# Places of two groups of SBUF tiles written out in tables instead of left to pools of three and of six

## The chip, the cores and the metric

One core of a Trainium2 chip runs the kernel. The metric is device time in microseconds (us) of one execution; lower is better. The engines are named as the profile names them: PE (matrix products; PEld is its weight load), DVE (vector), ACT (scalar), POOL (GpSimd) and SP, whose queue issues all the DMAs of this kernel in the order of the program.

## The reference

A recurrent attention over 768 steps feeds a gated dense part (batch 4, 8 heads of 40, model width 320, inner width 1024):

```python
for t in range(S):                       # state: [B, H, 40, 40]
    y[:, :, t] = einsum('bhd,bhde->bhe', r_t, state)
    Sa = einsum('bhde,bhe->bhd', state, a_t)
    state = state * w_t - einsum('bhd,bhe->bhde', Sa, b_t) + einsum('bhd,bhe->bhde', v_t, k_t)
x = y as [batch, time, 320]
h = gelu_tanh(x @ w_in); u, v = halves of h
v_n = (v - mean) / sqrt(var + 1e-6) * g_ln
v_s = einsum('ts,bsd->btd', w_sg, v_n) + b_sg
out = x + (u * v_s) @ w_out
```

All is 32-bit floating point, with `w_in` and `w_out` handed over as 64-bit numbers.

## The kernel before

**Attention.** Time is cut into 12 chunks of 64 steps. For each chunk the gates, a triangular inverse of size 64 and a chain of small products over the four batches run. The inverse is a long row of small products and sums `th<-x,n`, `x<-x,th` on POOL (tiles `tg` and `th` in turn from chunk to chunk), finished by a few instructions on DVE (`x<-x,n`) and two transposes (`x1z<-x`, `xt<-x1z`). Results go to DRAM (`xd<-yt`), from where the dense part reads them.

**Dense part.** It starts while the last chunks of the attention run. Its weights come first: `split64` (lines 1026 to 1066) takes one block of 128 x 256 numbers of 64 bits through these steps: `load` (DMA into a stage tile `stg`), `size` (ACT, `sc<-stg`), `fields` and `scale` (DVE, on `sc`, `lt`, `stg`), `parts` (ACT, `lt<-lt` and `wih<-stg`), `low` (three instructions on DVE or on POOL, the last of them `wil<-stg,lt`). `weights_in` lists twelve such blocks of `w_in`, `part_out` eight of `w_out`. The end of `low` is the last use of a block's stage tile.

**Order.** Every instruction is kept in program order on its engine (class `InOrder`), so ACT, DVE, POOL and SP each work through a fixed list, and an instruction that waits holds up all that stands behind it. Times in tables place each step in that list: `DEC` gives each of the twelve blocks its time and whether DVE (0) or POOL (1) does `low`; `DSTEP` gives the distances of its six steps:

```python
DSTEP = ((-15.76, -2.54, -1.13, -0.3, 1.65, 2.2), (-13.56, -0.46, 1.98, 3.41, 7.44, 12.01))
DEC = ((268.49, 0), (278.24, 0), (290.42, 0), (291.86, 0), (282.12, 1), (294.83, 1), (305.79, 1), (316.12, 0),
    (310.87, 0), (320.78, 1), (326.62, 0), (327.2, 1))
```

Sorted by the time of `load`, the blocks are those with index 0, 1, 4, 2, 3, 5, 6, 8, 7, 9, 10, 11. So POOL does `low` of the third, sixth, seventh, tenth and twelfth block that is loaded, DVE that of the others.

**Places.** A stage tile comes from `stage` (line 1007), out of a group of three equal places; the temporary tiles (`sc`, `lt` of `split64`; `p`, `q` of `gelu2`) come from `tmp` (line 1004), out of six. A new tile has to wait until the tile that had its place before is used for the last time. Which place a tile gets is decided where the program is put together, not in the source. There are 20 stage tiles and 152 temporary ones. The banks of PSUM are given out otherwise: class `Banks` reads the place of each tile from a table, `BANK`.

Of the kernel before, what the change touches and what calls it, by code (L numbers as in the profile page):

```python
# [24 lines left out]
HF = DF // 2  # L25
# [94 lines left out]
    1000.0, 1000.0, 1000.0)  # L120
HEADX = (1000.0, 13.61, -7.08, 1000.0, 4.3, 5.34, 13.95, 11.71, 1000.0, 1000.0, 6.17, 4.08, 1000.0, 8.27, 26.21, 8.84,
    3.72, 15.74, 23.09, 1000.0, 10.42, -4.32, 14.21, 1000.0)
BANK = ("0123450123435501250453111055152145231023102310214320321405302453145321045301502402315034310243524305"
        "1243154102103541323510234023145023452410413524303541032103425103235034134250321253412041230541202512"
        "3423051204052340134021534015412312054103051230423014523040530120145304245012431240351243523013045234"
# [13 lines left out]
class Banks:  # L139


    def __init__(self, tc, ctx):
        self.tc, self.ctx, self.n = tc, ctx, 0
        self.pools = [self.bank(i) for i in range(6)]
# [13 lines left out]
    def __call__(self, nm):  # L158
        k = int(BANK[self.n]) if self.n < len(BANK) else self.n % len(self.pools)
        self.n += 1  # L160
        return self.pools[k].tile([128, 512], F32, tag="ps", name=nm)
# [17 lines left out]
def engines(tc):  # L179
    nc = tc.nc  # L180
    return tuple(InOrder(tc, e) for e in (nc.vector, nc.scalar, nc.gpsimd, nc.tensor, nc.sync))
# [6 lines left out]
def attention(tc, a, xd, flag, keep, ps, mlp=None):  # L188
# [4 lines left out]
    with ExitStack() as ctx:  # L193
# [586 lines left out]
        def loads(f, stage, c, bs, *a):  # L780
            assert all((stage, c, b) in seen for b in bs)
            f(*a)
# [147 lines left out]
class Mlp:  # L930
# [3 lines left out]
    def __init__(self, tc, ps, xd, w_in, w2, g_ln, wst, b_sg, w_out, out):  # L934
        self.tc, self.ps, self.xd, self.out = tc, ps, xd, out
        self.w_in, self.w2, self.g_ln, self.wst, self.b_sg, self.w_out = w_in, w2, g_ln, wst, b_sg, w_out
        self.V, self.A, self.G, self.T, self.Q = engines(tc)
        self.ctx = ExitStack()
        self.vn, self.us, self.gs, self.xin, self.left, self.outs = {}, {}, {}, {}, [8] * B, {}
        self.ready = set()  # L940
        self.n, self.todo, self.plan, self.hold, self.held = 0, [], None, None, {}
# [60 lines left out]
        self.ut.update({(f, 1): p.tile([128, 384], F32, name=f"u{4 + f}") for f in range(4)})  # L1002

    def tmp(self, nm, n, dt=F32):
        return self.sb.tile([128, HF], dt, name=nm, tag="pq", bufs=6)[:, 0:n]

    def stage(self, n, dt):
        return self.sb.tile([128, HF], dt, name="stg", tag="stg", bufs=3)[:, 0:n]

    def later(self, *steps):  # L1010

# [314 lines left out]
    def run(self, ahead, verdict=None):  # L1326

        done = [(x, b) for x, b, _ in FILL] if ahead else []
        seq, jobs = [], []
        if not ahead:  # L1330
            self.ps.grow()
            self.open_in()
            for g in self.weights_in():
                for f in g(self.G):
                    f()
            self.open_x()
            self.open_v()
            self.open_sg()
        self.open_rest()
        for b in range(B):  # L1340
            seq += [(x, b + (x[0] in "uvx")) for x in (SEQL if b == B - 1 else SEQ)] if b else list(SEQ0)
        seq = [x for x in seq if x[1] < B and x not in done and (ahead or x[0][0] != "j")]
        for i, (x, b) in enumerate(seq):
            if x[0] == "x" and (b or not ahead) and not (ahead and (x, b) == ("x0", 1) and PX1):
                jobs.append((max(0, i - XL), lambda b=b, n=int(x[1]): self.load_x(b, n)))
            if verdict and (x, b) == ("s7", 1):
                jobs.append((i, lambda: self.later((8, 9, verdict()))))
        rest, loads, parts, wo = self.weights_rest([(i % 6, i // 6) for i, _ in SGA] if ahead else [])
        jobs += [(REST - 3, rest[0]), (REST, rest[1])]
        for k, f in enumerate(loads):  # L1350
            if f:
                jobs.append((SGS[k - 5] if k > 4 else 0, f))
        for k, f in enumerate(parts):
            if f:
                jobs.append((SGS[k], f))
        for k, g in enumerate(wo):
            for d, f in zip(OSTEP, g):
                jobs.append((OUTS[k] + d, f))
        jobs.sort(key=lambda x: x[0])
        for i, (x, b) in enumerate(seq):  # L1360
            while jobs and jobs[0][0] <= i:
                jobs.pop(0)[1]()
            self.piece(x, b)
        self.flush()
        self.ctx.close()
# [111 lines left out]
```

## Time and profile before

| | |
|---|---|
| median of 3 runs | 610.83 us (609.41 to 615.5) |
| the profiled execution | 612.37 us |
| its span, first to last instruction | 610.6 us |
| mean granted clock of PE | 0.959 |
| busy share: PE, DVE, POOL, ACT | 93%, 80%, 60%, 59% |
| chain that ended last, by engine | PE 62%, DVE 16%, POOL 7%, ACT 5%, issue 4%, DMA 3% |

The profile is that of one execution. Busy shares are means over the whole span. The page also gives the busy share in 40 slices of 15.3 us: PE stands at nine tenths or more in most of them, at six tenths in the slice from 305 to 321 us. The chain that ended last is followed back from the last instruction, at each step to what released it. "SPq" is SP's queue of DMAs.

### The profile page before, as it was taken

Reading aid. Unit: us, or ns where it says so; the run is one execution under the profiler, and the core shown is the slowest. Engines: PE = TensorE matmul, PEld = TensorE weight load, DVE = VectorE, ACT = ScalarE, POOL = GpSimd, SP = SyncE. Lnnn points to the kernel's source line nnn. Section 1 sums busy time; section 2 is a strip of 40 time slices with the busy share of each in tenths; the row PEclk is TensorE's granted clock in tenths of the full one; section 3 lists DMA queues with packets and bytes.
Section 4 is the critical chain, followed back from the end, with each engine's and each line's share of the span. In section 5 each row is a group of like instructions: output and inputs, shape, how many; then the busy total and the mean of one; then the engine's idle time right before and its main releaser. Section 6 shows DMA issues by size and latency. Waiting matters only on the chain.

```text
span 610.6 us, 23787 instructions
## 1 busy us (share of the span) xinstructions
PE 566.4 (93%) x9784; PEld 515.1 (84%) x9784; DVE 489.5 (80%) x1083; ACT 359.0 (59%) x993; POOL 363.5 (60%) x844
## 2 busy tenths in 40 slices
PE   6777999999999999999968989699999999999996
PEld 5666888888888888888857879699899999999996
DVE  7868999999989999997846887898887779568733
ACT  5546788797787887976826737444453246224410
POOL 7648888888888798888871344355433332333230
PEclk9875999999999999999897999799999999999999
DMA  5522335444454345525405415500121103010002
GB/s 204 151 66 83 91 100 138 132 122 120 123 138 126 98 127 137 137 73 139 123 10 149 113 51 158 166 29 5 34 73 38 34 1 110 2 33 13 20 1 71
DMA packets 56886, 54.01 MB, mean 88 GB/s; under 512 B 35840, under 2 KB 47360, under 8 KB 56768
## 3 DMA queue, kind: packets, MB, share of 16 engines
q1 hardware_dynamic: 56768, 52.40, 30.7%
q8 instruction: 79, 1.29, 0.9%
q14 instruction: 39, 0.32, 0.2%
HBM read 44.52 MB, written 7.86 MB: 86 GB/s over the span
## 4 chain that ended last, share of the span: by engine, by line
PE 62%; DVE 16%; POOL 7%; ACT 5%; issue 4%; DMA 3%; SPq 0%; DVEq 0%; POOLq 0%; ACTq 0%
PE sg L174 12%; PE ru L174 8%; PE ab L174 7%; PE op L174 6%; PE hu L174 6%; PE pq L174 5%; PE yp L174 5%; PE hv L174 4%; PE sp L174 3%; POOL x L174 3%; DVE at L174 2%; POOL th L174 2%; PE ut L174 2%; DVE fixed L174 2%; DVE ex L174 2%
## 5 line engine op out<-in xcount | busy, mean ns | idle before, releaser
L174 POOL TENSOR_TENSOR th<-x,n 128x126 f32<-128x126 f32 (+21 forms) x174 | 65.5, 376 | 21.6 <-DVE n L174 10.5
L174 POOL TENSOR_TENSOR x<-x,th 128x126 f32<-128x126 f32 (+21 forms) x174 | 69.1, 397 | 8.2
L174 PE MATMUL sg<-wsh,vh 128*128 128x384 f32 x192 | 66.0, 344 | 4.5 <-ACT wsh L174 4.5
L174 POOL TENSOR_TENSOR gx<-g,gy 128x384 fp32r<-128x384 f32 x30 | 31.8, 1063 | 64.5 <-ACT gy L174 64.5
L174 PE MATMUL sg<-wsl,vh 128*128 128x384 f32 x192 | 65.8, 342 | 0.4 <-POOL wsl L174 0.4
L174 PE MATMUL sg<-wsh,vl 128*128 128x384 f32 x192 | 65.7, 342 | 0.0
L174 POOL TENSOR_TENSOR tg<-x,n 128x126 f32<-128x126 f32 (+25 forms) x160 | 57.3, 358 | 12.3 <-DVE n L174 5.0
L174 POOL TENSOR_TENSOR x<-x,tg 128x126 f32<-128x126 f32 (+25 forms) x160 | 60.2, 376 | 7.1
L174 PE MATMUL pq<-rt,vut 128*64 128x128 f32 x768 | 52.6, 278 | 1.2 <-issue 1.1
L174 PE MATMUL ab<-at,kb 64*64 64x64 f32 x1536 | 39.6, 233 | 11.3 <-POOL kb L174 3.6
L174 ACT CAST gy<-g 128x384 fp32r<-128x384 f32 x30 | 15.4, 514 | 55.4 <-DVE g L174 52.7
L174 PEld LDWEIGHTS pq<-rt,vut 128*64 128x64 f32 x768 | 43.3, 139 | 3.9 <-issue 2.2
L174 ACT CAST vh<-v 128x512 fp32r<-128x512 f32 x24 | 14.9, 621 | 53.3 <-DVE v L174 53.3
L174 PEld LDWEIGHTS ab<-at,kb 64*64 64x64 f32 x1536 | 32.7, 141 | 15.3 <-POOL kb L174 4.0
L174 DVE TENSOR_TENSOR at<-ab,mask 64x256 f32<-64x256 f32 x96 | 40.4, 421 | 5.4 <-PE ab L174 2.9
L174 POOL TENSOR_TENSOR vl<-v,vh 128x512 fp32r<-128x512 f32 x24 | 31.5, 1311 | 20.8 <-ACT vh L174 20.8
L174 PEld LDWEIGHTS sg<-wsh,vh 128*128 128x128 f32 x192 | 37.0, 193 | 5.3 <-ACT wsh L174 4.8
L174 DVE SCALAR_TENSOR_TENSOR g<-sg,gl,bt 128x384 f32<-128x384 f32 x32 | 19.7, 615 | 25.3 <-PE sg L174 24.2
L174 POOL TENSOR_TENSOR rs<-rs,mhalf 128x1 f32<-128x1 f32 x24 | 13.2, 550 | 42.1 <-DVE rs L174 40.1
L174 PEld LDWEIGHTS sg<-wsl,vh 128*128 128x128 f32 x192 | 36.9, 192 | 1.0 <-POOL wsl L174 0.8
L174 DVE TENSOR_TENSOR pqs<-pq,mask 128x512 f32<-128x512 f32 x48 | 32.4, 677 | 6.1 <-PE pq L174 5.9
L174 PEld LDWEIGHTS sg<-wsh,vl 128*128 128x128 f32 x192 | 36.9, 192 | 0.0
(169 smaller groups left out, 1712.7 us busy)
## 6 DMA issues: line engine op xcount, KB each, us to landing
main<-main SPq DMA_DIRECT2D x88, 160.8 KB
vs<-vb SPq DMA_DIRECT2D x24, 160.0 KB
vu<-vs SPq DMA_DIRECT2D x24, 160.0 KB
rt<-rt SPq DMA_DIRECT2D x48, 80.0 KB
vut<-vt SPq DMA_DIRECT2D x24, 160.0 KB
xd<-yt SPq DMA_DIRECT2D x96, 40.0 KB
xt<-xd SPq DMA_DIRECT2D x16, 192.0 KB
out<-y SPq DMA_DIRECT2D x16, 192.0 KB
```

The source lines that it names most:

```text
L174: return self.tc.keep_in_program_order(f(*a, **k))
```

## The change

`tmp` and `stage` no longer take a tile from one group of six or three places. They look up the tile's number, in the order in which the program asks for tiles, in a table (`TMP`, `STAGE`) and take a group of one place that has that number in its name. The second, sequential version of the dense part (`run(False)`, which does not run with these inputs) sets `turns` to `None` and keeps the pools. Sizes and number of places stay, and no computation, DMA or order is edited.

```diff
+TMP = ("0123450123021345023514023541354103524105342013524105342510421530421534051243051423015240351243015240"
+        "3152403514230152430514203152403152430514203154230512")
+STAGE = ("01201012021012012012")
@@ class Mlp, __init__
+        self.turns = {}
@@
     def tmp(self, nm, n, dt=F32):
-        return self.sb.tile([128, HF], dt, name=nm, tag="pq", bufs=6)[:, 0:n]
+        if self.turns is None:
+            return self.sb.tile([128, HF], dt, name=nm, tag="pq", bufs=6)[:, 0:n]
+        k = self.turn("pq", TMP, 6)
+        return self.sb.tile([128, HF], dt, name=nm, tag=f"pq{k}", bufs=1)[:, 0:n]
 
     def stage(self, n, dt):
-        return self.sb.tile([128, HF], dt, name="stg", tag="stg", bufs=3)[:, 0:n]
+        if self.turns is None:
+            return self.sb.tile([128, HF], dt, name="stg", tag="stg", bufs=3)[:, 0:n]
+        k = self.turn("stg", STAGE, 3)
+        return self.sb.tile([128, HF], dt, name="stg", tag=f"stg{k}", bufs=1)[:, 0:n]
+
+    def turn(self, nm, table, bufs):
+        i = self.turns.get(nm, 0)
+        self.turns[nm] = i + 1
+        return int(table[i]) if i < len(table) else i % bufs
@@ run(self, ahead, ...), if not ahead:
+            self.turns = None
```

## Rows read from the trace of the kernel before

**Rows 1.** Busy time by stretch: PE, PEld, DVE, ACT, POOL; PEclk; DMA; GB/s.

```profile
315.00:320.00 5.00, 0.00 (x0) 0.00 (x0) 0.00 (x0) 0.00 (x0) 3.42 (x8) 0.81 0.02 5
320.00:325.00 5.00, 1.99 (x30) 1.66 (x32) 2.49 (x10) 2.91 (x10) 0.00 (x0) 0.50 0.68 198
```

**Rows 2.** Chain that ended last, around the hole: start, us, what.

```profile
318.08 0.74 POOL wil L174
...
318.84 3.03 DMA stg<-w
```

**Rows 3.** Timeline of SP's queue: start, us, DMA, idle time before it.

```profile
290.59 0.40 SPq L174 DMA_DIRECT2D stg<-w_in  x1
292.42 0.36 SPq L174 DMA_DIRECT2D stg<-w  x1
...
302.86 0.62 SPq L174 DMA_DIRECT2D vut<-vt  x1
318.84 0.36 SPq L174 DMA_DIRECT2D stg<-w  x1
...
326.04 0.37 SPq L174 DMA_DIRECT2D stg<-w  x1
...
327.64 0.36 SPq L174 DMA_DIRECT2D stg<-w_in  x1
```

**Rows 4.** Timeline of ACT: start, us, instruction, idle time before it and its releaser.

```profile
311.48 0.29 ACT L174 COPY s<-ru 80x160 f32<-80x160 f32 x1
321.95 0.43 ACT L174 ACTIVATE sc<-stg 128x256 f32<-128x256 f32 x1 [10.18 <-DMA stg<-w]
...
332.09 0.44 ACT L174 ACTIVATE sc<-stg 128x256 f32<-128x256 f32 x1
```

**Rows 5.** Timeline of PE, same columns.

```profile
314.08 0.68 PE L174 MATMUL ru<-rhsb,xt 64*64 64x64 f32 x16
323.01 0.86 PE L174 MATMUL ut<-ident,vu 64*80 64x64 f32 x4 [8.25 <-ACT vu L174]
...
326.66 1.87 PE L174 MATMUL pq<-rt,vut 128*64 128x128 f32 x16
328.36 0.44 PE L174 MATMUL sp<-sc,ident 128*64 128x80 f32 x8
...
329.04 1.20 PE L174 MATMUL gp<-x1z,nts 32*32 32x32 f32 x64
...
335.99 1.05 PE L174 MATMUL pq<-rt,vut 128*64 128x128 f32 x16
```

**Rows 6.** Timeline of DVE, same columns.

```profile
309.43 0.49 DVE L174 TENSOR_TENSOR wil<-stg,lt 128x256 fp32r<-128x256 f32 x1
...
322.41 0.62 DVE L174 TENSOR_SCALAR sc<-sc 128x256 f32<-128x256 f32 x2 [10.11 <-ACT sc L174]
...
324.38 0.69 DVE L174 SCALAR_TENSOR_TENSOR x<-x,n 128x15 f32<-128x15 f32 x3
325.10 1.09 DVE L174 STREAM_TRANSPOSE x1z<-x 128x512 f32<-128x512 f32 x1
...
332.56 0.62 DVE L174 TENSOR_SCALAR sc<-sc 128x256 f32<-128x256 f32 x2 [1.66 <-ACT sc L174]
```

**Rows 7.** Timeline of POOL: end of the last inverse, and of the third block's `low`.

```profile
316.35 0.27 POOL L174 TENSOR_TENSOR x<-x,th 128x45 f32<-128x45 f32 x1
...
318.08 0.73 POOL L174 TENSOR_TENSOR wil<-stg,lt 128x256 fp32r<-128x256 f32 x1
```

**Rows 8.** Timeline of POOL: same 17 instructions in two inverses, first and last of each.

```profile
263.61 0.34 POOL L174 TENSOR_TENSOR th<-x,n 128x78 f32<-128x78 f32 x1
...
268.35 0.35 POOL L174 TENSOR_TENSOR tg<-x,n 128x96 f32<-128x96 f32 x1
...
288.28 0.39 POOL L174 TENSOR_TENSOR tg<-x,n 128x78 f32<-128x78 f32 x1
...
293.76 0.35 POOL L174 TENSOR_TENSOR th<-x,n 128x96 f32<-128x96 f32 x1
```

## The prediction

> **What bounds the kernel now.** I read the page's 40 slices first: PE is full nearly everywhere except around 305 to 321 us. Then busy time by stretch: from 315 to 320 PE, DVE and ACT do nothing at all, and only POOL works [rows 1]. A hole in which three engines stop together is one late signal, so I read the chain that ended last across it. It runs over POOL's `wil<-stg,lt`, ends that at 318.82, waits 3.03 us for the DMA of a stage tile [rows 2], and goes on with ACT's `sc<-stg` at 321.95 [rows 4]. The reader is to see that the DMA is issued 0.02 us after POOL is done: it waited for that place.
>
> The timeline of SP's queue says since when. Its DMA before the late one is over at 302.86 + 0.62 = 303.48, and then SP does nothing until 318.84 [rows 3]: 15.4 us at the head of a list that must keep its order. It is the sixth load of a block; the third and fourth were issued at 290.59 and 292.42 [rows 3], the first, second and fifth stand between and before and are left out.
>
> Whose place was it? By the order of `DEC`, POOL does `low` of the third block, loaded at 290.59 [rows 3], and POOL had first to end a whole inverse, at 316.35 + 0.27 = 316.62 [rows 7]. The fourth block, done by DVE, gave up its place at 309.43 + 0.49 = 309.92 [rows 6]. So the sixth load stood behind the third block's tile while the fourth's was free for 8.9 us. The rest is a chain of queues: ACT has nothing after 311.48 + 0.29 = 311.77 but a wait of 10.18 us [rows 4]; DVE waits 10.11 for ACT [rows 6]; PE ends at 314.08 + 0.68 = 314.76 and waits 8.25 for ACT's `vu`, which stands behind `sc` [rows 5].
>
> **The change part by part.** *Stage table.* It begins 0 1 2 0 1 0 1 2 0. The sixth tile takes place 0 after the fourth, not place 2 after the third. The seventh follows the fifth, the eighth (place 2) follows the third, the ninth the sixth. From the tenth on each follows a tile loaded two to four before it, about as a turn of three would have it; I cost these at nothing either way. A load that reaches SP's head after its place is free waits for nothing, and one that waited for the block three before still does.
>
> *Temporary table.* It starts 0 to 5 and 0 1 2 3, as a turn of six would, and then departs. None of the idle times in [rows 4 to 6] is released by the last use of a temporary tile. One place matters: five blocks take tiles 0 to 9, so the sixth block's `sc` is tile 10. A turn of six would put it behind tile 4, the third block's `sc`, which POOL reads in `low`, after 316.62. The table puts it behind tile 6, the fourth block's `sc`, done before 309.92. So the two tables belong together, and this one by itself is worth nothing; as bounds I take 0.3 us either way, less than one DVE instruction on a whole block [rows 6].
>
> *Sixth load, the term that counts.* It can start at 309.95. Its DMA takes 3.03 as before [rows 2], so ACT's `sc` runs at about 313.05 in place of 321.95: 8.9 us earlier. What is late next?
>
> PE: its `ut` came 323.01 - 321.95 = 1.06 after `sc`, which now is 314.1, and PE itself is busy until 314.76. The wait of 8.25 is gone whole [rows 5]. Behind it PE ran at half clock: the granted clock was 0.50 in that stretch, the level of 1.2 GHz, after PE had done nothing since 314.76 [rows 1]. At that level `pq` takes 1.87, at the other 1.05 [rows 5], a ratio of 0.56. The stretch from 323.01 to 328.36 is 5.35 and would be 3.0 at full clock, 2.35 saved. With both, PE could reach `gp` up to 10.6 earlier than 329.04.
>
> POOL does not move: its inverse ends at 316.62 whatever the load does. DVE's `x<-x,n` needs it, and stood at 324.38 [rows 6]; 8.9 earlier would be 315.5, so it now waits until 316.7. That is one new wait, on DVE, of 1.2 us, with the transposes and all of DVE behind it. `x1z` ends 325.10 + 1.09 - 324.38 = 1.81 after `x` starts [rows 6], at 318.5.
>
> POOL also gets company. DVE stood still beside its last steps and will work now. Two rows price that: the same 16 instructions from 78 to 96 columns took 268.35 - 263.61 = 4.74 in one chunk and 293.76 - 288.28 = 5.48 in the one in which DVE decodes a weight block [rows 8], 0.74 more, 16%. The sixth block runs only half of such a decoding beside the inverse. Between nothing and 0.74 I take 0.4: POOL's inverse ends at 317.0, `x1z` at 318.9. PE's `gp`, which reads it, then starts at 318.9 and not 329.04: 10.1 earlier.
>
> Of the page SBUF — State Buffer (section SBUF: two separate sides), the Trainium skill says that DVE and GpSimd share a pair of ports under an exclusive lock, the loser blocked for the whole instruction. The 16% agree with some blocking; taken in full, the rule gives the first rival below.
>
> *Eighth load, the new wait.* SP issued it at 326.04 [rows 3], 7.2 after the sixth, so it reaches SP's head at about 317.2 and must wait for the third block's `low` on POOL, over at 318.81 [rows 7], with 0.4 more 319.2. Behind it on SP stand stores of `yt` and the ninth load, then loads for the next chunk. The ninth needs POOL's `low` of the sixth block, three instructions of some 0.73 right behind the third's [rows 7]: 321.4, against 327.64 [rows 3]. That is only 6.2 earlier, but SP then waited for DVE anyway. The eighth tile is read by ACT's `sc` at 332.09 [rows 4]. Its data land at 319.2 + 0.03 + 3.03, so ACT can start at 322.35: 9.7 earlier. This is later than what PE allows (10.1) and so it sets the gain. DVE lost more at `x`, but at 332.56 it waits 1.66 for this same `sc` [rows 6], which swallows the difference.
>
> *The sum.* Earlier by 9.7 at this point; 0.2 off for new semaphores and the small order of things: 9.5. All that follows is released by work behind the hole, and no engine holds back a piece of work begun before it, so the shift stays to the end. Against its own time: 612.37 - 9.5 = 602.9. The profiled execution lies 1.54 above the median, so 610.83 - 9.5 = 601.3.
>
> **The rivals.** *POOL becomes the late one.* If each DVE instruction that now runs beside POOL blocks it for its whole length, the work from 322.41 to 324.38 (2.0 us) falls on the inverse, and `x` and a transpose (0.69 + 1.09 = 1.8) on `low` [rows 6]. The eighth tile's place then comes free at 318.81 + 3.8 = 322.6 and ACT's `sc` starts at 325.7, 6.4 earlier: 604.4. Against it: 0.74 measured over 5.5 us in which DVE decoded a block [rows 8]. [...]
>
> *The hole was cover.* DVE is busy most of the time after 345, and if its work there were bound by something that does not move, the gain would go there: 610.8. The sixth load could also still wait for something that these rows do not name, with the same time; so could a table that gives the old places. Against all: the places read off the table differ from those in rows 3, and the chain crosses the hole.
>
> *Slower.* The new wait of the eighth load sits at the head of SP. It costs nothing as long as its data land before 332.09, so as long as POOL releases the place before 329.0, 10.2 later than now. POOL's work between 313.05 and 318.81 is 5.8 us and would have to take 2.8 times as long; released 16 us later, the kernel is slower by some 6: 617. Measured is 1.16 times [rows 8].
>
> **How the numbers follow.** Chances: forecast 0.77, POOL late 0.12, no gain 0.08, slower 0.03. A measurement of this kernel tells about 1% from no change, 6.1 us, so the bound is 604.7. The forecast's own range is a gain of 8 to 10.6 with 1.4 of scatter below (610.83 - 609.41): 598.8 to 604. The second case with scatter above reaches 606.5, and 1 in 10 is left beyond. Faster by over 1%: 0.75 from the forecast and 0.07 from the second case, which lies at the bound, 0.82. Within 1%: the rest of these two and the third, 0.15. Slower: 0.03.
>
> **What would show it.** In the profile after, the sixth load starts just behind a `wil` of DVE near 310; ACT's wait of 10.18 shrinks to about 1.3; PE goes from `ru` to `ut` without a wait and stays at full clock; DVE shows a new wait before `x<-x,n`, released by POOL; SP's wait for POOL moves to the eighth load, near 319. The prediction is wrong if the sixth load is still released by POOL, if POOL's inverse ends after 318, or if the stretches behind 350 are not earlier by the same amount.

## The result: about half of the forecast gain

The changed kernel takes 605.86 us (median of 20 runs, 602.71 to 609.86) against 610.63 (20 runs, 607.37 to 617.03): a ratio of 0.9919, 95% interval 0.9893 to 0.9946. That is 4.8 us less, where 9.5 were forecast. The time is inside the stated range (598.8 to 606.5), near its upper end and outside the forecast's own part of it (598.8 to 604). The gain of 0.8% is within 1%, to which the prediction gave 0.15, against 0.82 for more. Ratios and intervals, here and below, leave out the few runs in a slower state of the chip, while medians are of all runs. The profiled execution took 607.05, its span is 605.3 and the mean granted clock of PE 0.963.

In all rows, L174 and L177 are the line of the helper through which each operation goes, in the kernel before and in the changed one. Busy time by stretch in the changed kernel: PE, PEld, DVE, ACT, POOL; PEclk (the clock granted to PE, as a share of 2.4 GHz); DMA; GB/s. The stretch in which three engines stood still [rows 1] is full of work now, but PE has 2 us of idle time in it, and behind it the clock is low.

```profile
315.00:320.00 5.00, 2.94 (x88) 2.82 (x84) 3.09 (x7) 2.87 (x9) 4.45 (x11) 1.00 0.59 136
320.00:325.00 5.00, 4.02 (x94) 3.51 (x96) 4.14 (x11) 2.51 (x6) 1.90 (x3) 0.63 0.49 137
325.00:330.00 5.00, 5.00 (x94) 4.25 (x90) 1.84 (x6) 3.09 (x9) 0.00 (x0) 0.69 0.17 42
```

SP's queue in the changed kernel (start, us, DMA): the sixth load at 309.73, the eighth at 319.82.

```profile
303.00 0.64 SPq L177 DMA_DIRECT2D vut<-vt  x1
309.73 0.37 SPq L177 DMA_DIRECT2D stg<-w  x1
...
319.82 0.37 SPq L177 DMA_DIRECT2D stg<-w  x1
```

The sixth load goes 0.03 us after DVE's `wil` of the fourth block (309.17 + 0.53, below) and no longer after POOL's of the third. It was at 318.84 [rows 3], so it is 9.1 earlier.

ACT in the changed kernel (start, us, instruction, idle time before it and its releaser): `sc` of the sixth block, and of the eighth.

```profile
312.98 0.43 ACT L177 ACTIVATE sc<-stg 128x256 f32<-128x256 f32 x1 [1.50 <-DMA stg<-w]
...
325.40 0.44 ACT L177 ACTIVATE sc<-stg 128x256 f32<-128x256 f32 x1
```

The wait of 10.18 [rows 4] is 1.50. The eighth block's `sc` has no wait in front of it: its data were there.

POOL, DVE and PE in the changed kernel, same columns, one fence for each. POOL:

```profile
313.88 0.34 POOL L177 TENSOR_TENSOR th<-x,n 128x78 f32<-128x78 f32 x1
314.30 1.04 POOL L177 TENSOR_TENSOR x<-x,th 128x78 f32<-128x78 f32 x1
...
317.33 0.28 POOL L177 TENSOR_TENSOR x<-x,th 128x45 f32<-128x45 f32 x1
317.56 0.73 POOL L177 TENSOR_TENSOR lt<-lt,sc 128x256 f32<-128x256 f32 x1
318.25 0.73 POOL L177 TENSOR_TENSOR stg<-stg,wih 128x256 f32<-128x256 f32 x1
319.06 0.73 POOL L177 TENSOR_TENSOR wil<-stg,lt 128x256 fp32r<-128x256 f32 x1
```

DVE:

```profile
309.17 0.53 DVE L177 TENSOR_TENSOR wil<-stg,lt 128x256 fp32r<-128x256 f32 x1
...
314.72 0.41 DVE L177 SCALAR_TENSOR_TENSOR stg<-stg,sc 128x256 int32<-128x256 int32 x1
...
317.63 2.20 DVE L177 SCALAR_TENSOR_TENSOR x<-x,n 128x15 f32<-128x15 f32 x3 [1.81 <-POOL x L177]
319.87 1.06 DVE L177 STREAM_TRANSPOSE x1z<-x 128x512 f32<-128x512 f32 x1
```

PE:

```profile
314.41 0.42 PE L177 MATMUL ut<-ident,vu 64*80 64x64 f32 x4
...
317.46 0.47 PE L177 MATMUL sp<-vu,kbt 128*40 128x40 f32 x16
320.98 1.71 PE L177 MATMUL gp<-x1z,nts 32*32 32x32 f32 x64 [3.04 <-DVE x1z L177]
...
326.46 1.88 PE L177 MATMUL xp<-xt,gs 64*32 64x32 f32 x64
```

Three things are to be seen. One instruction of POOL's inverse takes 1.04, while the one before it on as many columns takes 0.34. DVE's three `x<-x,n` take 2.20 where they took 0.69 [rows 6]. And PE, which has no wait left before `ut` (8.25 before [rows 5]), has a new one of 3.04 before `gp`, and runs behind it at half clock: `gp` takes 1.71 where it took 1.20 [rows 5], `xp` 1.88 where it took 1.20:

```profile
332.35 1.20 PE L174 MATMUL xp<-xt,gs 64*32 64x32 f32 x64
```

(That row is from PE's timeline of the kernel before.) The chain that ended last in the changed kernel (start, us, what) now crosses the place like this:

```profile
317.33 0.28 POOL x L177
317.61 0.02 issue
317.63 1.39 DVE x L177 x2
319.03 0.02 issue
319.05 0.79 DVE x L177
319.84 0.02 issue
319.87 1.07 DVE x1z L177
320.94 0.04 issue
320.98 1.71 PE gp L177 x64
```

No DMA is left in it. It goes from the inverse on POOL over DVE to PE.

**A common zero.** Spans also hold what happened earlier in an execution; in the eleven profiles the end of the fourth block's `wil` on DVE lies between 307.9 and 313.4. The table counts from there, a point that the change cannot move. "POOL" is the start of POOL's `x<-x,th` on 120 columns, some 2.5 us ahead of the zero; "inverse" is the end of POOL's last `x<-x,th`, "x" the time of DVE's three `x<-x,n`, "gp" and "xp" the start of these products on PE, "end" the end of the span. The names in the lower rows are those of the experiments.

| kernel | POOL | inverse | x | gp | xp | end |
|---|---|---|---|---|---|---|
| before | -2.77 | 6.70 | 0.69 | 19.12 | 22.43 | 300.7 |
| after | -2.30 | 7.90 | 2.20 | 11.28 | 16.76 | 295.6 |
| stage table alone | -2.30 | 7.2 | 1.23 | 15.26 | 18.57 | 296.6 |
| temporary table alone | -2.78 | 6.72 | 0.69 | 19.05 | 22.36 | 302.6 |
| `low` of two blocks on DVE | -2.31 | 8.18 | 0.69 | 10.03 | 14.84 | 293.2 |
| products on PE in the wait | -2.30 | 8.05 | 2.24 | 11.62 | 14.93 | 293.4 |
| decoding behind the inverse | -2.31 | 7.19 | 2.20 | 10.56 | 16.02 | 294.8 |
| before, third block's `low` on DVE | -2.31 | 8.17 | 2.19 | 11.53 | 17.21 | 295.6 |
| `low` on DVE and decoding late | -2.30 | 7.38 | 0.70 | 9.26 | 14.23 | 294.1 |
| the same and products | -2.32 | 7.39 | 0.69 | 9.65 | 13.76 | 293.4 |
| `low` on DVE and products | -2.77 | 7.71 | 0.70 | 10.38 | 13.69 | 292.0 |

By this zero the change brings 300.7 - 295.6 = 5.1 us, close to the 4.8 of the medians.

The column "POOL" shows that the profiles are of two kinds. In those of the kernel before, of the temporary table alone and of the last row POOL is 0.5 us further on, before anything that the change touches; in the others, the one without tables among them, it is not. The rows of POOL before and after:

```profile
307.15 0.44 POOL L174 TENSOR_TENSOR x<-x,th 128x120 f32<-128x120 f32 x1
```

```profile
307.40 0.71 POOL L177 TENSOR_TENSOR x<-x,th 128x120 f32<-128x120 f32 x1
```

The first starts 309.92 - 307.15 = 2.77 ahead of its zero, the second 309.70 - 307.40 = 2.30. Why executions differ in this is open. Within a kind the column agrees to 0.02; between the kinds some 0.5 us of a difference can be this. From the start of DVE's last `y` to the end there are 4.9 to 5.3 us in all profiles but one, so "end" is good to some 0.3.

### The profile page after: what moved, and what is told of

It reads as the page before. It is cut to its first block, busy times and chain, and to the rows that moved or that the text cites. A ratio compares the mean times of both kernels' runs of the same rounds, so it can differ in the third digit from the quotient of the medians.

```text
span 605.3 us, 23787 instructions
## 1 busy us (share of the span) xinstructions
PE 567.2 (94%) x9784; PEld 516.1 (85%) x9784; DVE 491.3 (81%) x1083; ACT 358.7 (59%) x993; POOL 364.1 (60%) x844
## 4 chain that ended last, share of the span: by engine, by line
PE 60%; DVE 20%; POOL 8%; ACT 6%; issue 5%; DMA 1%; SPq 0%; POOLq 0%; DVEq 0%; ACTq 0%
PE sg L177 12%; PE ru L177 7%; PE op L177 6%; PE ab L177 6%; PE hu L177 6%; PE pq L177 4%; PE yp L177 4%; PE hv L177 4%; POOL x L177 3%; DVE at L177 3%; POOL th L177 2%; PE sp L177 2%; PE wp L177 2%; DVE fixed L177 2%; DVE sc L177 2%
## 5 line engine op out<-in xcount | busy, mean ns | idle before, releaser
L177 POOL TENSOR_TENSOR th<-x,n 128x126 f32<-128x126 f32 (+21 forms) x174 | 66.1, 380 | 21.3 <-DVE n L177 10.9
L177 POOL TENSOR_TENSOR x<-x,th 128x126 f32<-128x126 f32 (+21 forms) x174 | 69.1, 397 | 8.1
L177 POOL TENSOR_TENSOR gx<-g,gy 128x384 fp32r<-128x384 f32 x30 | 31.7, 1060 | 64.5 <-ACT gy L177 64.5
L177 PE MATMUL sg<-wsh,vh 128*128 128x384 f32 x192 | 65.7, 342 | 4.5 <-ACT wsh L177 4.5
L177 PE MATMUL sg<-wsl,vh 128*128 128x384 f32 x192 | 65.4, 341 | 0.4 <-POOL wsl L177 0.4
L177 PE MATMUL sg<-wsh,vl 128*128 128x384 f32 x192 | 65.5, 341 | 0.0
L177 POOL TENSOR_TENSOR tg<-x,n 128x126 f32<-128x126 f32 (+25 forms) x160 | 57.5, 359 | 12.8 <-DVE n L177 5.5
L177 POOL TENSOR_TENSOR x<-x,tg 128x126 f32<-128x126 f32 (+25 forms) x160 | 60.3, 377 | 7.0
L177 PE MATMUL pq<-rt,vut 128*64 128x128 f32 x768 | 51.4, 275 | 0.6 <-issue 0.6
L177 PE MATMUL ab<-at,kb 64*64 64x64 f32 x1536 | 39.6, 234 | 10.5 <-POOL kb L177 3.6
L177 ACT CAST gy<-g 128x384 fp32r<-128x384 f32 x30 | 15.4, 515 | 55.4 <-DVE g L177 52.2
L177 ACT CAST vh<-v 128x512 fp32r<-128x512 f32 x24 | 14.9, 621 | 53.1 <-DVE v L177 53.1
L177 PEld LDWEIGHTS pq<-rt,vut 128*64 128x64 f32 x768 | 42.5, 137 | 2.9 <-issue 1.2
L177 PEld LDWEIGHTS ab<-at,kb 64*64 64x64 f32 x1536 | 32.8, 142 | 14.3 <-POOL kb L177 4.0
L177 DVE TENSOR_TENSOR at<-ab,mask 64x256 f32<-64x256 f32 x96 | 40.4, 421 | 5.1 <-PE ab L177 2.7
L177 POOL TENSOR_TENSOR vl<-v,vh 128x512 fp32r<-128x512 f32 x24 | 31.5, 1313 | 20.6 <-ACT vh L177 20.5
L177 PEld LDWEIGHTS sg<-wsh,vh 128*128 128x128 f32 x192 | 36.8, 192 | 5.4 <-ACT wsh L177 4.8
L177 DVE SCALAR_TENSOR_TENSOR g<-sg,gl,bt 128x384 f32<-128x384 f32 x32 | 19.7, 614 | 25.4 <-PE sg L177 24.4
L177 POOL TENSOR_TENSOR rs<-rs,mhalf 128x1 f32<-128x1 f32 x24 | 13.2, 550 | 42.1 <-DVE rs L177 40.1
L177 PEld LDWEIGHTS sg<-wsl,vh 128*128 128x128 f32 x192 | 36.6, 191 | 1.0 <-POOL wsl L177 0.8
L177 DVE TENSOR_TENSOR pqs<-pq,mask 128x512 f32<-128x512 f32 x48 | 32.3, 675 | 6.4 <-PE pq L177 6.2
L177 PEld LDWEIGHTS sg<-wsh,vl 128*128 128x128 f32 x192 | 36.7, 191 | 0.0
```

The source lines that it names most:

```text
L177: return self.tc.keep_in_program_order(f(*a, **k))
```

## The experiments

The theory: the whole gain is the one place behind which SP stood, and what is missing went to two losses of their own, POOL and DVE holding each other up around `x<-x,n`, and PE's clock after the new wait. The rivals: one of the tables does it alone, the losses come with the tables, or they hide each other, so that taking one away brings nothing. The first two experiments part the tables, the next three take away one suspected loss each, the sixth does without tables, and the rest put the losses together.

**Stage table alone.** `tmp` goes back to its group of six:

```diff
-        k = self.turn("pq", TMP, 6)
-        return self.sb.tile([128, HF], dt, name=nm, tag=f"pq{k}", bufs=1)[:, 0:n]
+        return self.sb.tile([128, HF], dt, name=nm, tag="pq", bufs=6)[:, 0:n]
```

> The stage table alone; the temporary tiles stay in the pool of six. Theory A (the two tables belong together): the sixth load starts near 309.9 us and lands near 313, but its tile sc is number 10 and has the place of the third block's sc, which POOL reads in low until about 317.3; so ACT waits for POOL and its sc starts near 317.5, and DVE's lt of that block waits for POOL's wil near 318.8. PE's gp starts near 321.8 and the time is 606 to 607.5. Theory B (the stage table is the whole change): ACT's sc starts at 313 and the time is that of the changed kernel, 605.9.

Measured: 607.66, ratio 0.9924 (0.9879 to 0.9968). ACT's timeline at the sixth block's `sc`:

```profile
319.09 0.43 ACT L177 ACTIVATE sc<-stg 128x256 f32<-128x256 f32 x1 [6.12 <-POOL lt L177]
```

The load is early, but `sc` waits for POOL's `lt<-lt,sc`, the first instruction of the third block's `low` and the last to read that block's `sc`. So the sixth block's `sc` stands in the place of the third block's when the pool gives it out, as the prediction read off the order. Here PE waits 4.20 before `ut` and has a granted clock of 0.50 from 320 to 325; `gp` starts at 15.26 from the zero, where the expected 321.8 would be some 12. From the common zero the kernel gains 4.1, 1.0 less than with both tables; the ratios can't tell the two apart.

**Temporary table alone.** `stage` goes back to its group of three:

```diff
-        k = self.turn("stg", STAGE, 3)
-        return self.sb.tile([128, HF], dt, name="stg", tag=f"stg{k}", bufs=1)[:, 0:n]
+        return self.sb.tile([128, HF], dt, name="stg", tag="stg", bufs=3)[:, 0:n]
```

> The table of the temporary tiles alone; the stage tiles stay in the pool of three. Theory A: the sixth load is released by POOL's wil near 318.8 as before, the hole stays, 610.6. Theory B (places of the temporary tiles cost something in the dense part as well): faster by 1 us or more with the hole unchanged.

Measured: 615.13, ratio 1.0058 (1.0016 to 1.0100). ACT and PE at the hole:

```profile
320.05 0.43 ACT L177 ACTIVATE sc<-stg 128x256 f32<-128x256 f32 x1 [10.18 <-DMA stg<-w]
...
321.11 0.86 PE L177 MATMUL ut<-ident,vu 64*80 64x64 f32 x4 [8.25 <-ACT vu L177]
```

Both waits are the same to a hundredth as in [rows 4] and [rows 5]: this table by itself takes nothing from the hole. Neither theory had the loss of 0.6%, which is clear of the noise. It has no place in the dense part, where from the zero on DVE stays within 0.4 us of the kernel before; in this profile it lies at the end, where from the start of DVE's last `y` to the end of the span there are 7.15 us and not 4.94. In the changed kernel, which has the same table, these are 4.99. Whether that end also makes the medians is open.

**`low` of the third and sixth block on DVE**, with both tables. POOL then has nothing to do beside DVE's `x<-x,n`:

```diff
-  steps[k] = self.weights_in()[k](self.G if DEC[k][1] else self.V)
+  steps[k] = self.weights_in()[k](self.G if DEC[k][1] and k not in (4, 5) else self.V)
```

> The changed kernel, with the last step (low) of the third and the sixth block on DVE in place of POOL, at the same places in the program. Theory A (POOL's low blocks DVE's three x<-x,n, which took 2.20 us in place of 0.69, and that late gp costs PE a wait of 3.0 and its full clock): the three take about 0.7 to 0.9, gp starts about 1.5 earlier, PE waits about 1.5; the time is 604.4 if PE's clock still falls there and 601.5 if it does not. Theory B (the three are slow for another reason): they still take 2.2 us and gp stays near 321, and the time is 605.9 or, with more work on DVE, longer.

Measured: 604.14, ratio 0.9875 (0.9802 to 0.9948). DVE, PE, and the stretch from 320:

```profile
319.73 0.69 DVE L177 SCALAR_TENSOR_TENSOR x<-x,n 128x15 f32<-128x15 f32 x3 [2.23 <-POOL x L177]
...
321.55 1.20 PE L177 MATMUL gp<-x1z,nts 32*32 32x32 f32 x64 [1.79 <-DVE x1z L177]
```

```profile
320.00:325.00 5.00, 3.45 (x96) 2.97 (x98) 4.86 (x14) 2.60 (x6) 0.00 (x0) 0.79 0.40 92
```

The three sums take 0.69 again with POOL idle. So it was POOL's `low` that held them. The end comes 2.4 earlier than with the change alone.

**Useless products on PE in the new wait**, with both tables. Eleven products without a reader stand in front of the last chunk's `gp`:

```diff
         def inv_g(c):
             nt, x1z = nts[c % 3], x1_of[c]
+            if c == NCH - 1:
+                mlp.fill(11)
@@ class Mlp
+    def fill(self, n):
+        p = self.ps
+        o = p.pools[int(BANK[p.n])].tile([128, 512], F32, tag="ps", name="fill")
+        for _ in range(n):
+            self.T.matmul(o, lhsT=self.wih[:, 0, HF:HF + 128], rhs=self.wih[:, 0, HF:DF], start=True, stop=True,
+                          skip_group_check=True)
```

> The changed kernel with 11 products of no use (about 3.0 us) put ahead of gp of the last chunk on PE, into the bank that gp takes. Theory A (the wait before gp costs its 3.0 us and then some 2.9 us of PE at half clock): the granted clock stays at 1.0 from 318 to 330, gp still starts near 321, xp ends about 2.5 earlier, the time is 603 to 603.5. Theory B (the half clock is hidden behind other engines): the clock stays, but the time is 605.9 as in the changed kernel.

Measured: 602.0, ratio 0.9841 (0.9796 to 0.9885), the only interval that lies below that of the change itself. PE, and the stretch from 320:

```profile
321.43 2.79 PE L177 MATMUL fill<-wih 128*128 128x512 f32 x11
324.56 1.20 PE L177 MATMUL gp<-x1z,nts 32*32 32x32 f32 x64 [0.34 <-DVE sc L177]
...
327.87 1.20 PE L177 MATMUL xp<-xt,gs 64*32 64x32 f32 x64
```

```profile
320.00:325.00 5.00, 4.66 (x80) 3.84 (x78) 3.90 (x7) 1.81 (x6) 4.69 (x9) 1.00 0.47 120
```

The granted clock stays at 1.00, the level of 2.4 GHz. `gp` starts no earlier than in the changed kernel, 0.34 later even, and still the end comes 2.2 earlier. So the half clock behind the new wait is a loss of its own.

**Decoding of the sixth block behind the inverse**, with both tables. DVE's `fields` and `scale` of that block come later:

```diff
-  for i, d in enumerate(DSTEP[DEC[k][1]]):
+  for i, d in enumerate((-13.56, -0.46, 6.3, 6.5, 7.44, 12.01) if k == 5 else DSTEP[DEC[k][1]]):
```

> The changed kernel, with the sixth block's fields and scale on DVE moved behind the last steps of the inverse (x<-x,n, x1z), all else in place. Times from the end of the fourth block's wil. Theory A (DVE's decoding beside POOL's inverse makes it late: end at 7.9 in place of 6.7 in the kernel before): the inverse ends at 6.7 to 6.9 and x<-x,n starts 1.0 earlier; the three still take about 2.2 beside POOL's low, gp starts at 10.2 to 10.4 in place of 11.3, and the time is 1 to 2.5 shorter than that of the changed kernel, about 604. Theory B (the inverse is late for another reason): it ends at 7.9 and gp stays at 11.3.

Measured: 605.82, ratio 0.9894 (0.9858 to 0.9930). POOL, then PE:

```profile
314.86 0.34 POOL L177 TENSOR_TENSOR x<-x,th 128x78 f32<-128x78 f32 x1
```

```profile
320.83 1.70 PE L177 MATMUL gp<-x1z,nts 32*32 32x32 f32 x64 [2.32 <-DVE x1z L177]
```

The instruction of 1.04 takes 0.34 when DVE does not decode beside it, and the inverse ends 0.7 earlier, at 7.19, as it does with the stage table alone. Expected were 6.7 to 6.9, after the kernel before; the rest of the way to its 6.70 is the 0.5 by which POOL is further on there already ahead of the zero. The end moves by no more than 0.8: PE still waits 2.32, and the clock still falls. The medians don't show the gain (605.82 against 605.86).

**No table: the kernel before, with the third block's `low` on DVE.** The place that the sixth load waits for then comes free early in the old order too:

```diff
-  steps[k] = self.weights_in()[k](self.G if DEC[k][1] else self.V)
+  steps[k] = self.weights_in()[k](self.G if DEC[k][1] and k != 4 else self.V)
```

> The kernel before, with its two pools, and the low of the third block on DVE in place of POOL. Theory A (the hole is the third block's tile held until POOL is through its inverse, and nothing else): the sixth load is released near 303 to 310 and not by POOL, the wait of ACT for the stage tile is below 2 us, and the time is at least as short as that of the changed kernel, 603 to 606. Theory B (the tables bring something beyond that one place): the hole is gone but the time stays 2 us or more above the changed kernel, 608 or more.

Measured: 604.48, ratio 0.9875 (0.9813 to 0.9936). ACT, then PE:

```profile
312.15 0.44 ACT L174 ACTIVATE sc<-stg 128x256 f32<-128x256 f32 x1 [1.40 <-DMA stg<-w]
```

```profile
320.49 1.92 PE L174 MATMUL gp<-x1z,nts 32*32 32x32 f32 x64 [3.29 <-DVE x1z L174]
```

The hole is gone with no table, and the new wait and the half clock are there as well. The end from the zero is the same, 295.6. So in these profiles what the tables bring is this one wait, and the two losses come with its removal and not with them.

**Both moves together:** `low` of the two blocks on DVE and the decoding late.

> The changed kernel with both edits: low of the third and sixth block on DVE, and the sixth block's fields and scale behind x<-x,n. Times from the end of the fourth block's wil. Theory A (both pairs of engines get in each other's way, and that is what the change lost): POOL's inverse ends near 7.0 to 7.4, x takes 0.7, gp starts near 9.0, PE waits 1 us or less and keeps its full clock; the end comes 8 to 9 us earlier than in the kernel before, 601 to 602.5. Theory B (the lost part went to something else): gp at 10 or later and no better than with low on DVE alone.

Measured: 603.71, ratio 0.9873 (0.9815 to 0.9930). PE, and a stretch:

```profile
322.61 1.20 PE L177 MATMUL gp<-x1z,nts 32*32 32x32 f32 x64 [1.01 <-DVE x1z L177]
...
327.58 1.95 PE L177 MATMUL xp<-xt,gs 64*32 64x32 f32 x64
```

```profile
325.00:330.00 5.00, 4.89 (x101) 4.26 (x98) 4.68 (x16) 4.54 (x12) 0.00 (x0) 0.50 0.34 84
```

`gp` starts at 9.26, the earliest of all, but the clock falls at 324.3 for 6.8 us and `xp` takes 1.95. The end, 294.1, is later than that of the first move alone (293.2). Theory A had the inverse, `x` and the shorter wait right, and missed that the clock falls all the same; the end comes 6.6 earlier than in the kernel before, not 8 to 9.

**The same with five products in front of `gp`.**

> All three edits together: low of the third and sixth block on DVE, the sixth block's scale after the end of the inverse, and five useless products on PE in front of the last chunk's gp. Theory A (what the run with the first two edits lost again was the fall of PE's granted clock at 324.3, for 6.8 us): the clock stays at 1.0 from the inverse to 15 us behind it, gp starts about 9.3 us after the end of the fourth block's wil, xp 3.3 behind gp (before: 3.3, after: 5.5), the last instruction about 291.2 us after that wil against 294.05 without the products, ratio near 0.982. Theory B (the earlier gp runs into another wait, on ACT or DVE, which holds the dense part): the clock stays up, but the last instruction is again 293 to 294 us behind the wil, ratio 0.985 to 0.988.

Measured: 604.31, ratio 0.9866 (0.9805 to 0.9927). The clock is 1.00 from 310 to 330, but `xp` comes late:

```profile
322.46 0.25 PE L177 MATMUL xp<-xt,gs 64*32 64x32 f32 x2 [0.21 <-ACT gs L177]
323.06 1.20 PE L177 MATMUL xp<-xt,gs 64*32 64x32 f32 x62 [0.36 <-ACT gs L177]
```

Here the second theory holds. PE waits for ACT's `gs`, and from `gp` to `xp` it is 4.11 at full clock, against 3.31 in the kernel before and 4.97 in the run without products. The end is 293.4: the clock's fall was not the only thing that the seventh run lost.

**`low` on DVE with eight products in front of `gp`.**

> Two edits: low of the third and sixth block on DVE, and eight useless products on PE in front of the last chunk's gp. Theory A (DVE's three sums and PE's clock are separate losses that add): x<-x,n takes 0.7 us, the clock stays at 1.0 behind the inverse, gp starts about 10.2 us after the end of the fourth block's wil and xp 3.3 behind it, the last instruction about 291.9 us after the wil (with low on DVE alone 293.2, with the products alone 293.4), ratio near 0.983. Theory B (one hides the other): the last instruction no earlier than 293 us after the wil.

Measured: 604.8, ratio 0.9864 (0.9799 to 0.9929). DVE, then PE:

```profile
315.68 0.70 DVE L177 SCALAR_TENSOR_TENSOR x<-x,n 128x15 f32<-128x15 f32 x3 [1.81 <-POOL x L177]
316.41 1.12 DVE L177 STREAM_TRANSPOSE x1z<-x 128x512 f32<-128x512 f32 x1
```

```profile
316.16 2.10 PE L177 MATMUL fill<-wih 128*128 128x512 f32 x8
318.32 1.20 PE L177 MATMUL gp<-x1z,nts 32*32 32x32 f32 x64
...
321.63 1.31 PE L177 MATMUL xp<-xt,gs 64*32 64x32 f32 x64
```

The end is at 292.0 (expected 291.9), 8.7 earlier than in the kernel before, a profile of the same kind: most of the forecast 9.5 is there. It is 3.6 earlier than with the change, where the two savings by themselves are 2.4 and 2.2. Some 0.5 of the 3.6 is the kind of the profile, so the hit on 291.9 is in part luck, and the savings add only in part. One reason shows: the eight products outlast the wait, as `x1z` ends at 316.41 + 1.12 = 317.53 and `gp` starts at 318.32. In medians this version can't be told from the others; their spread is wider than what is left to gain.

## Why the prediction was right, and where half of the gain went

**Right in the mechanism.** The cause of the hole, the new place of the sixth load (309.73, forecast 309.95), ACT's wait (1.50, forecast about 1.3), the end of PE's wait before `ut`, the new wait on DVE for POOL (1.81, forecast 1.2), and that the shift stays: DVE is ahead of the kernel before by 5.21 at 338.7 and by 5.35 at its last `y`. The new wait of the eighth load is the one that was named, 0.8 later from the zero than it was put (319.82, forecast 319.2). The stage table alone takes only part of the hole away, the temporary table alone nothing, so it takes both; that the second is worth 1.0 us is seen in the profiles, not in the medians.

**In the time, partly luck.** The forecast was 601.3 and its own range ended at 604; 605.86 lies inside the stated range only because that goes up to 606.5, 2.1 above the 604.4 of the first rival. The prediction works these 2.1 out from no row, and the rival's chain of events is not what happened, as shown below. No run shows the 0.2 that the sum takes off for semaphores and order either.

**Wrong by size: the way from the inverse to `gp`.** The prediction had `gp` at 318.9 with the fourth block's `wil` ending at 309.92, which is 8.98 from the zero. Measured is 11.28. The 2.3 us are three terms, of which the first two show at the end of the inverse:

- 0.5 that is not the change: the profile of the changed kernel is of the kind in which POOL is that much less far on already ahead of the zero.
- "Between nothing and 0.74 I take 0.4" for what DVE's decoding costs POOL's inverse. Measured: 7.90 against 7.19 with the decoding moved away, so 0.7, 0.3 more than taken, and nearly all of it in the one instruction of 1.04. The two inverses of [rows 8] were a poor measure: DVE is busy for 3.68 of the 4.74 us beside the faster one too, so they compare decoding with other work of DVE, and not with none.
- "`x1z` ends 1.81 after `x` starts". Measured: 319.87 + 1.06 - 317.63 = 3.30, 1.5 more. This step failed. The prediction looked for DVE holding up POOL and put no price on POOL holding up DVE. The second and the third `x<-x,n` end 0.04 to 0.05 after an instruction of POOL's `low`: the chain has ends at 319.02 and 319.84, POOL's rows end at 318.25 + 0.73 = 318.98 and 319.06 + 0.73 = 319.79. With POOL idle the three take 0.69. DVE reached `x` 6.75 earlier (317.63 against 324.38 [rows 6]), while POOL's `low` moved by less than 1 us, and so the two met.

The Trainium skill's page SBUF — State Buffer (section SBUF: two separate sides) has an exclusive lock between a DVE instruction with two inputs in SBUF and a POOL instruction that reads SBUF: it goes to whichever of the two starts first, and the other is blocked for the whole instruction. The trace agrees for `x<-x,n`, whose ends follow POOL's; that POOL was first it shows clearly for the first of the three alone (317.56 against 317.63), as the third starts within 0.01 of POOL's instruction. The prediction took this rule one way only, with POOL blocked each time, and called that the rule in full. The transpose `x1z`, which has one input and runs beside POOL's next instruction, takes 1.06, and 1.09 before [rows 6], and so isn't held.

**Wrong outright: "stays at full clock".** The prediction put `ut` at 314.1 and `gp` at 318.9 and took the clock's gain of 2.35 from the old place, but did not ask whether PE has work in between. Its sum has no term for a fall of the clock behind `gp`, and no reason for leaving it out. PE was idle for 3.04, and the granted clock was 0.5 (1.2 GHz) from 321.3 to 328.1. From `gp` to `xp` it is 16.76 - 11.28 = 5.48 where it was 22.43 - 19.12 = 3.31: 2.2 lost, and 0.6 more behind `xp`. The products in the wait show it without argument: `gp` 0.34 later, full clock, and 2.2 earlier at the end.

**Wrong, without weight: the eighth load as the one that sets the gain.** ACT's `sc` of that block came at 325.40 and waited for nothing, since ACT got there only after PE's `ru`, which PE worked through late and at half clock.

**The sum, mended.** From the zero, `gp` would have been 10.1 earlier; 2.3 less on the way to it, 2.2 less from `gp` to `xp` and 0.6 less behind it leave 5.1, which is what the profiles show. As 0.5 of the 2.3 is the kind of the profile, the change is worth some 5.6 by estimate between profiles of one kind. The first rival named the right pair of engines, but with POOL as the late one: it had the eighth load wait until 322.6, and it went at 319.82. The claim that the temporary table by itself is worth nothing within 0.3 holds at the hole and not in the medians (1.0058), and there the cause is open.

## What to carry to other kernels

When a hole is closed, write down which instructions of two engines run beside each other in the new order, and price it both ways round: a small instruction of DVE on the path can be held by a long one of POOL that used to run alone. Then look for the idle time that PE has left and price the clock behind it, which here cost 2.8 us behind a wait of 3.04. And before a difference of two profiles is put down to the change, see whether the engines stood alike ahead of it; here half a microsecond did not belong to it. A wait at the head of a queue can be removed by a tile's place or by the engine that releases it; both brought the same here.

## What the runs showed of the hardware that was not expected

- Small DVE instructions beside POOL's: `x<-x,n` of 8 to 16 columns has a median of 252 ns over the kernel and a longest of 778. The row groups the changed kernel's instructions of that form (ns least, median and longest; first and last start in us):

```profile
L177 DVE SCALAR_TENSOR_TENSOR x<-x,n x34: 236/252/778, 36.6 to 319.1; 128x15 f32<-128x15 f32 x22, 128x16 f32<-128x16 f32 x11, 128x8 f32<-128x8 f32 x1
```

- The granted clock fell for 6.8 us after an idle time of PE of 3.04 in the changed kernel, for 3.4 after 1.79 with `low` on DVE, and again for 6.8 after one of only 1.01 with both moves. The shortest wait thus had no shorter fall. What the fall cost differs: 2.8 us in the changed kernel, but with both moves the end came only 0.7 earlier when products kept the clock up (294.1 and 293.4), as ACT's `gs` held PE there in any case.
- Longer runs of one kernel mostly have a lower mean granted clock over the whole span: with the eleven products, four runs took 601.0 to 602.3 at 0.968 to 0.971, two 608.0 at 0.959 and 0.961. In the profile of one of these two the clock fell at 71.2 for 6.8 us, far ahead of the change. It isn't so for each run: the changed kernel also took 603.73 at 0.961 and 607.18 at 0.965. That is why the losses here are read from a common zero.
